# Second pass of an attention and mixer kernel: relus two products later, three raw results in other tiles, weights rounded earlier, weight sums spread over two groups

## The chip, the cores and the metric

The kernel runs on one core of a Trainium2 chip. Five engines work beside each other, each through its own queue in order: TensorE (PE; its weight loads are PEld), VectorE (DVE), ScalarE (ACT), GpSimd (POOL) and SyncE (SP), which here issues the DMAs. Matrix products go from SBUF to PSUM; the other engines empty PSUM and add tiles in SBUF. The metric is the time of one launch on the device in microseconds (us). [...]

## The reference, cut to what matters

```
# attention: q, k, v are (8, 8, 576, 64)
kv  = einsum('bhsd,bhse->bhde', k, v)
out = einsum('bhsd,bhde->bhse', q, kv)
out = out / sqrt(mean(out * out, -1) + 1e-6) * g_norm
x   = out.transpose(0, 2, 1, 3).reshape(8, 576, 512)
# mixer
h = relu(x.T @ w_tok1) @ w_tok2      # over the tokens, 576 -> 256 -> 576
u = x + h.T
return u + relu(u @ w_ch1) @ w_ch2   # over the channels, 512 -> 1536 -> 512
```

The four weights are given as 64-bit floats, the rest is 32-bit.

## The kernel before, in words

**First pass (0 to about 254 us).** Attention and token mixing for pairs of batches; u goes to DRAM (`u_dram`). The order on each engine is chosen by a scheduler from the order in which the code is written and from its own costs, so the diff does not show it. In the same stretch the weights come in as pairs of 32-bit words and are rounded to 32-bit floats by `decode` (lines 142 to 165), one block of 128 rows at a time. There are 16 blocks of `w_ch1` and 12 of `w_ch2`. A block is one DMA into a tile `raw` (three turn), one instruction of ScalarE (line 154), two of GpSimd (155, 165) and four of VectorE (157, 159, 161, 163). The steps of the blocks are woven among the steps of the pass (`weave`, line 632): fetch of a block ahead of the rounding of the block before it.

**Second pass (254 us to the end).** Nine groups of 512 tokens (the ninth holds the last 64 tokens of all eight batches) go through the channel mixer: u @ w_ch1, relu, @ w_ch2. All instructions that go through `keep` (line 111) stay in the order of the code on their engine. The products are done by Winograd's form of Strassen's scheme: 7 products of blocks, called by their numbers in the order 1, 6, 7, 5, 2, 3, 4, in place of 8, with sums of blocks ahead of and behind them.

- `channel1_once` (line 429), group 0: one level of the scheme, in 3 parts, 21 products.
- `channel1` (line 490), groups 1 to 8: two levels. Each of seven outer products `o` is itself seven inner products, the functions `first` (1), `sixth`, `seventh`, `fifth`, `second`, `fourth`, `third`. An inner product is 3 matmuls of 128x128 into a PSUM tile of the pool `m`, which has six. Behind it ScalarE copies it (`t1`, and the quarter `dst(0, 0)`) or VectorE adds it (`u2`, `u3` and the other three quarters of the result).
- The result of an outer product is a raw tile `v` or `vs`: a11, a12, a22, s1 to s4 (printed as v11, v12, v22, vs1 to vs4). GpSimd adds such tiles to each other (`padd`, six sums of 128x1536 a group). ScalarE takes relus of a11, a22 and a12 in place, and VectorE then forms s1, s2, s3, s4 (`v_sums`, `v_sum3`), the operands of channel2.
- `channel2` (line 572): 7 products, the operands `V[g]`, results added into `xg` by VectorE; the transposes of the next group's u (`prepare`) stand between its products.

A relu is put into ScalarE's queue not where its sum is, but in the last step of the next outer product (`later`, lines 496 and 564):

```
            def third():
                product(3, "p5", False, True)
                tensor_add(dst(0, 1), at["p5"], at["u2"])
                while relus:
                    relus.pop()()
                after()
```

The two-level scheme needs sums of the weights: seven blocks `w2` for the outer level, made in the first pass, 28 sums for the inner level (`mix_ch1_of`, tile `w1`, in part in place in `w_ch1` and `w2`), and 8 sums of `w_ch2` (`mix_ch2`, tile `d2`). All are VectorE instructions. In group 0 the rounding of the last four blocks of `w_ch2` (with tiles of their own, `stage2`) and the 8 sums of `mix_ch2` are woven among the 21 products of `channel1_once`; the 28 sums stand behind the 7 steps of group 0's `channel2`, four behind each.

Of the kernel before, what the change touches and what calls it, by code (L numbers as in the profile page):

```python
# [9 lines left out]
F32 = mybir.dt.float32  # L10
# [7 lines left out]
def kernel(  # L18
# [123 lines left out]
    def decode(dst, raw):  # L142

        lo, hi = raw[..., 0], raw[..., 1]
        bits = dst.bitcast(U32)
        part = late.get("stage", stage).tile(list(dst.shape), F32, name="part", tag="part", bufs=2)
        keep(nc.scalar.activation(dst, hi.bitcast(F32), AF.Copy, scale=2.0 ** -112))
        nc.gpsimd.tensor_scalar(out=dst, in0=dst, scalar1=TOP, scalar2=-TOP,
                                op0=ALU.min, op1=ALU.max)
        keep(nc.vector.tensor_scalar(out=bits, in0=bits, scalar1=3, scalar2=None,
                                     op0=ALU.logical_shift_left))
        keep(nc.vector.scalar_tensor_tensor(out=bits, in0=hi, scalar=0x80000000, in1=bits,  # L159
                                            op0=ALU.bitwise_and, op1=ALU.bitwise_or))  # L160
        keep(nc.vector.tensor_scalar(out=part.bitcast(U32), in0=bits, scalar1=0xFF800000,  # L161
                                     scalar2=None, op0=ALU.bitwise_and))
        keep(nc.vector.scalar_tensor_tensor(out=part, in0=lo, scalar=2.0 ** -52, in1=part,  # L163
                                            op0=ALU.mult, op1=ALU.mult))
        nc.gpsimd.tensor_tensor(out=dst, in0=dst, in1=part, op=ALU.add)
# [4 lines left out]
    def block(n, loads, dst, turn=lambda raw: raw, home=None):  # L170

        raw = []

        def fetch():
            if home is None:
                raw.append(late.get("stage", stage).tile([P, n, 2], U32, name="raw", tag="raw", bufs=3))
            else:
                raw.append(home.tile([P, n, 2], U32, name="raw", tag="h1"))
            for o, i in loads(raw[0]):
                nc.sync.dma_start(o, i)  # L180

        return fetch, lambda: decode(dst, turn(raw[0]))
# [53 lines left out]

    def mix_ch2():

        steps = []
        for i in range(2):  # L240
            t1, t2, t4 = (late["d2"][:, n, ts(i, NS // 2)] for n in range(3))
            b11, b12, b21, b22 = (w_ch2[:, n, ts(i, NS // 2)] for n in range(4))
            steps.append([do(tensor_add, o, a, b, ALU.subtract)
                          for o, a, b in ((t1, b12, b11), (t2, b22, t1), (b12, b12, b22),
                                          (t4, b21, t2))])
        return [step for pair in zip(*steps) for step in pair]

    def w2_of(n):
        i = {1: 0, 7: 1, 2: 2, 3: 3}
# [240 lines left out]
    def channel1(g):  # L490

        a11, a12, a22, s1, s2, s3, s4 = v_blocks(g)
        padd = lambda o, a, b: tensor_add(o, a, b, engine=nc.gpsimd)
        relus = []

        def later(t):
            relus.append(do(relu, t, t))


        def after5():  # L500
            padd(s3, a22, s1)
            padd(a22, a22, a12)
            later(a22)

        def after2():
            padd(a11, a11, s2)
            later(a11)

        def after4():
            v_sums(s1, s2, s3, a11, a22)  # L510
# [4 lines left out]


        plan = {1: (a11, lambda: None), 6: (s1, do(padd, s1, s1, a11)),
                7: (a12, do(padd, a12, a12, s1)), 5: (a22, after5), 2: (s2, after2),
                3: (s4, do(padd, s3, s3, s4)), 4: (s4, after4)}

        def outer(o):
            to, after = plan[o]
# [30 lines left out]
            def second():  # L553
                product(2, "p1", False, True)
                copy(dst(0, 0), at["p1"])

            def fourth():
                product(4, "p7", False, True)
# [2 lines left out]
            def third():  # L561
                product(3, "p5", False, True)
                tensor_add(dst(0, 1), at["p5"], at["u2"])
                while relus:
                    relus.pop()()
                after()

            return [first, sixth, seventh, fifth, second, fourth, third]
# [89 lines left out]
    def run(order, *stages):  # L658
# [6 lines left out]
    tok = [get_tok1(0, 2), get_tok1(2, 2), get_tok1(4, 1)] + [get_tok2(t) for t in range(NTOK)]  # L665
    weights = ([get_ch1(c, f) for f in range(4) for c in range(NC)]
               + [get_ch2(f) for f in range(NF)])
    early, in_group = staggered(weights[:24]), staggered(weights[24:])
    cut = 38
    for fetch, _ in tok:  # L670
        fetch()
# [1 line left out]
    steps = []  # L673
    for pair in range(B // 2 - 1):
        steps += run(both, attention(pair + 1), token_mixing(pair))
    weave(steps, early[:cut])


    left.close()
# [2 lines left out]
    late["u"] = pool("u", 1)  # L682
    fetch_u(0)
    woven = []
    weave([do(woven.append, f) for f in early[cut:]],
          [do(woven.append, f) for f in mix_ch1()])
    steps = run(last, token_mixing(3))
    extra = prepare(0, lambda: ps["o"].tile([P, NC, P], F32, name="ps_ut", tag="o"))
# [8 lines left out]
    late["d2"] = pool("d2", 1, "right").tile([P, 3, NS, DH], F32, name="d2")  # L697
    late["m"] = pool("m", 6, space=bass.MemoryType.PSUM)
    late["t"] = pool("t", 2, space=bass.MemoryType.PSUM)
    for g in range(NG):  # L700
        fetch_u(g + 1)
        extra = prepare(g + 1, t_psum)
        if g == 0:
            with ExitStack() as late_stage:
                late["stage"] = pool("stage2", 2, "right", late_stage)
                weave(channel1_once(g), in_group + mix_ch2())
            late["w1"] = pool("w1", 1, "right").tile([P, 4, 3, FQ], F32, name="w1")
            sums = [mix_ch1_of(o) for o in ORDER]
        else:
            for step in channel1(g):  # L710
                step()
            sums = [[]] * 7
        for n, step in enumerate(channel2(g)):
            step()
            for f in extra[n:n + 1] + sums[n]:
                f()


# [33 lines left out]
```

## Time and profile before

| | |
|---|---|
| median of 3 runs | 943.27 us (940.22 to 946.04) |
| the profiled execution, time | 948.9 us |
| its span | 947.1 us |
| granted TensorE clock, mean | 0.971 |
| PE busy | 868.9 us, 92% |
| VectorE busy | 558.9 us, 59% |
| GpSimd busy | 273.0 us, 29% |
| ScalarE busy | 176.3 us, 19% |
| chain that ended last: PE / DVE / POOL | 63% / 17% / 10% |

The profile is of one execution; its span runs from the first instruction to the last, and the time of the execution is 1.8 us more. Its time lies 5.6 us above the median of the three runs. Busy shares are means over both passes: the rows of single stretches further below tell what binds where. An "idle before" is the time for which the engine had nothing running ahead of this group of instructions, with what ended most of it.

### The profile page before, as it was taken

The page shows a single profiled execution, that of the slowest core. Times are in us where ns is not written, and L with a number is a line of the kernel's source. Part 1 is how long each engine was busy: PE and PEld are TensorE (multiplying, and loading weights), DVE is VectorE, ACT ScalarE, POOL GpSimd, SP SyncE. Part 2 cuts the span into 40 slices and gives each one's busy share as a digit, 9 for nine tenths or more (in the row PEclk, how much of TensorE's full clock was granted, in tenths as well). Part 3 has the DMA queues.
Part 4 walks back from the last instruction along what each step waited for, and adds up shares of the span by engine and source line. Part 5 has one row for each costly group of instructions (what it writes and reads, how often), then busy time and mean ns, then how long its engine had stood idle before and what let it go on. Part 6 is the DMA issues. An engine that isn't in the chain of part 4 may idle for free.

```text
span 947.1 us, 12401 instructions
## 1 busy us (share of the span) xinstructions
PE 868.9 (92%) x5136; PEld 737.6 (78%) x5136; DVE 558.9 (59%) x862; ACT 176.3 (19%) x300; POOL 273.0 (29%) x144
## 2 busy tenths in 40 slices
PE   4699969879999988998999999899899899899897
PEld 4565555554587888898898889789789889889886
DVE  1868688786477664464554546536636546446551
ACT  2132222221121012112102202301211211210310
POOL 1534454552030017007106104303501600700710
PEclk9799979979999989999999999999999999999999
DMA  8787858624200020020011001002002002001001
GB/s 271 226 291 267 285 167 266 201 90 144 101 23 0 10 81 2 1 90 1 1 48 43 1 23 67 1 1 90 1 1 89 2 0 90 1 1 45 2 1 44
DMA packets 43576, 72.53 MB, mean 77 GB/s; under 512 B 2688, under 2 KB 21120, under 8 KB 43520
## 3 DMA queue, kind: packets, MB, share of 16 engines
q1 hardware_dynamic: 43376, 71.71, 22.8%
q8 instruction: 40, 0.66, 0.3%
q14 instruction: 16, 0.13, 0.0%
q10 hardware_dynamic: 144, 0.03, 0.0%
HBM read 52.85 MB, written 18.87 MB: 76 GB/s over the span
## 4 chain that ended last, share of the span: by engine, by line
PE 63%; DVE 17%; POOL 10%; issue 4%; DMA 3%; ACT 2%; POOLq 0%; SPq 0%; DVEq 0%; ACTq 0%
PE ps_w L124 33%; PE ps_v L124 21%; POOL vs L115 5%; POOL v L115 3%; PE ps_kv L266 2%; PE ps_u L345 2%; PE ps_h L327 2%; DVE w_ch L159 2%; PE ps_ut L378 2%; DVE part L161 1%; DVE ms L281 1%; DMA raw<-in_moe_w_ch_dram 1%; DVE x L294 1%; DVE part L163 1%; DVE u L115 1%
## 5 line engine op out<-in xcount | busy, mean ns | idle before, releaser
L124 PE MATMUL ps_v<-uT,w 128*128 128x128 f32 (+1 forms) x1656 | 221.6, 287 | 26.6 <-ACT t L121 18.1
L124 PEld LDWEIGHTS ps_v<-uT,w 128*128 128x128 f32 x1656 | 206.3, 197 | 33.6 <-ACT t L121 19.7
L115 POOL TENSOR_TENSOR vs<-vs,v 128x1536 f32<-128x1536 f32 x8 | 27.5, 3442 | 414.3 <-DVE vs L115 414.3
L124 PE MATMUL ps_v<-uT,w_ch 128*128 128x128 f32 (+1 forms) x864 | 126.6, 290 | 5.1 <-DVE u L115 5.1
L124 PEld LDWEIGHTS ps_v<-uT,w_ch 128*128 128x128 f32 x864 | 114.1, 195 | 9.4 <-DVE u L115 5.7
L124 PE MATMUL ps_w<-d,vs 128*128 128x256 f32 x432 | 96.2, 379 | 0.0
L124 PE MATMUL ps_w<-w_ch,v 128*128 128x256 f32 x432 | 96.2, 379 | 0.0
L124 PE MATMUL ps_w<-w_ch,vs 128*128 128x256 f32 x432 | 96.2, 379 | 0.0
L124 PEld LDWEIGHTS ps_w<-w_ch,vs 128*128 128x128 f32 x432 | 81.5, 190 | 10.7
L124 PEld LDWEIGHTS ps_w<-w_ch,v 128*128 128x128 f32 x432 | 80.8, 190 | 10.3
L124 PEld LDWEIGHTS ps_w<-d,vs 128*128 128x128 f32 x432 | 80.8, 190 | 10.3
L115 DVE TENSOR_TENSOR u<-ps_v,t 128x384 f32<-128x384 f32 (+1 forms) x59 | 33.3, 564 | 78.8 <-PE ps_v L124 44.2
L115 DVE TENSOR_TENSOR vs<-ps_v,u 128x384 f32<-128x384 f32 (+1 forms) x99 | 54.9, 561 | 39.8 <-PE ps_v L124 23.5
L266 PE MATMUL ps_kv<-v_in,k_in 128*128 128x128 f32 x320 | 49.4, 322 | 30.2 <-ACT kvp L270 20.9
L266 PEld LDWEIGHTS ps_kv<-v_in,k_in 128*128 128x128 f32 x320 | 46.6, 233 | 37.8 <-ACT kvp L270 24.1
L121 ACT COPY t<-ps_v 128x384 f32<-128x384 f32 (+1 forms) x59 | 28.4, 481 | 192.1 <-PE ps_v L124 192.1
L118 ACT ACTIVATE v<-v 128x1536 f32<-128x1536 f32 (+1 forms) x30 | 39.4, 1314 | 115.1 <-DVE v L115 83.9
L115 DVE TENSOR_TENSOR v<-ps_v,u 128x384 f32<-128x384 f32 (+1 forms) x78 | 44.3, 568 | 25.1 <-PE ps_v L124 19.9
L345 PE MATMUL ps_u<-h,w_tok 128*128 128x512 f32 x128 | 58.8, 603 | 0.0
L115 POOL TENSOR_TENSOR v<-v,vs 128x1536 f32<-128x1536 f32 x16 | 55.0, 3440 | 10.3 <-DVE v L115 10.3
L327 PE MATMUL ps_h<-x,w_tok 128*128 128x512 f32 x128 | 57.4, 595 | 0.3 <-POOL x L295 0.3
L295 POOL TENSOR_TENSOR x<-x,g_sb 128x1024 f32<-128x1024 f32 (+1 forms) x20 | 44.6, 2231 | 44.0 <-DVE x L294 28.9
(79 smaller groups left out, 977.5 us busy)
## 6 DMA issues: line engine op xcount, KB each, us to landing
qT<-in_q_dram SPq DMA_DIRECT2D x8, 1152.0 KB, 7.2
xg<-u_dram SPq DMA_DIRECT2D x9, 1024.0 KB, 5.7
k_in<-in_k_dram SPq DMA_DIRECT2D x16, 512.0 KB, 4.8
v_in<-in_v_dram SPq DMA_DIRECT2D x16, 512.0 KB, 6.3
u_dram<-x SPq DMA_DIRECT2D x16, 512.0 KB, 3.2
out_dram<-xg SPq DMA_DIRECT2D x16, 512.0 KB, 2.8
raw<-in_moe_w_ch_dram SPq DMA_DIRECT2D x16, 384.0 KB, 5.7
raw<-in_moe_w_ch_dram SPq DMA_DIRECT2D x12, 512.0 KB, 5.9
```

Source lines behind the costliest of these rows:

```text
L115: keep(engine.tensor_tensor(out=o, in0=a, in1=b, op=op))
L118: keep(nc.scalar.activation(o, a, AF.Relu))
L121: keep(nc.scalar.copy(o, a))
L124: keep(nc.tensor.matmul(*a, **kw))
L159: keep(nc.vector.scalar_tensor_tensor(out=bits, in0=hi, scalar=0x80000000, in1=bits, op0=ALU.bitwise_and, op1=ALU.bitwise_or))
L161: keep(nc.vector.tensor_scalar(out=part.bitcast(U32), in0=bits, scalar1=0xFF800000, scalar2=None, op0=ALU.bitwise_and))
L163: keep(nc.vector.scalar_tensor_tensor(out=part, in0=lo, scalar=2.0 ** -52, in1=part, op0=ALU.mult, op1=ALU.mult))
L266: nc.tensor.matmul(acc[:, i], lhsT=kk[:, j, ts(i, P)], rhs=vv[:, j, ts(i, P)], start=(j == 0), stop=(j == JJ - 1))
L295: nc.gpsimd.tensor_mul(x3, x3, g_sb.to_broadcast([P, n * H, D]))
L327: nc.tensor.matmul(acc[side, t], lhsT=w_tok1[:, j, ts(t, P)], rhs=x_of(pair, side * J + j), start=(j == 0), stop=False)
L345: nc.tensor.matmul(acc_u, lhsT=w_tok2[:, t, ts(i % J, P)], rhs=h1[i // J][:, t], start=(t == 0), stop=(t == NTOK - 1))
L378: keep(nc.tensor.transpose(pt[:, c], xg[g][:, i, ts(c, P)], ident))
```

## The change

Three things change, all in the order or place of work; the sums, products and relus are the same in number, and so are the bytes moved.

1. In `channel1` the result of o=5 goes to s3 in place of a22, that of o=2 to s4 in place of s2, and that of o=3 to s2 in place of s4. The two GpSimd sums behind o=5 change places: first a22 = s3 + a12, then s3 = s3 + s1. The relu of a22 is put in behind the second step of o=3 that fills `p1` (`second`), and that of a11 in the same step of o=4; before they were in the last step of o=2 and of o=3.
2. All 28 weight blocks are rounded in the first pass; none is left for group 0. The tiles `raw` and `part` of the last four come from the pool of the first pass.
3. Of the 8 sums of `mix_ch2`, four are woven into group 0's `channel1_once`. The other four and the 28 of `mix_ch1_of` make one list. Its first 24 are woven into group 0's `channel2` (its 7 steps and the 6 of `prepare`), the last 8, those of o=3 and o=4, into the first 18 of the 49 steps of group 1's `channel1`.

```
-        part = late.get("stage", stage).tile(list(dst.shape), F32, name="part", tag="part", bufs=2)
+        part = stage.tile(list(dst.shape), F32, name="part", tag="part", bufs=2)
...
-        steps = []
+        firsts, lasts = [], []
...
-            steps.append([do(tensor_add, o, a, b, ALU.subtract)
-                          for o, a, b in ((t1, b12, b11), (t2, b22, t1), (b12, b12, b22),
-                                          (t4, b21, t2))])
-        return [step for pair in zip(*steps) for step in pair]
+            sub = lambda o, a, b: do(tensor_add, o, a, b, ALU.subtract)
+            firsts += [sub(t1, b12, b11), sub(t2, b22, t1)]
+            lasts += [sub(b12, b12, b22), sub(t4, b21, t2)]
+        return firsts, lasts
...
         def after5():
-            padd(s3, a22, s1)
-            padd(a22, a22, a12)
-            later(a22)
+            padd(a22, s3, a12)
+            padd(s3, s3, s1)
+            relus.append((3, do(relu, a22, a22)))

         def after2():
-            padd(a11, a11, s2)
-            later(a11)
+            padd(a11, a11, s4)
+            relus.append((4, do(relu, a11, a11)))
...
-                7: (a12, do(padd, a12, a12, s1)), 5: (a22, after5), 2: (s2, after2),
-                3: (s4, do(padd, s3, s3, s4)), 4: (s4, after4)}
+                7: (a12, do(padd, a12, a12, s1)), 5: (s3, after5), 2: (s4, after2),
+                3: (s2, do(padd, s3, s3, s2)), 4: (s4, after4)}
...
             def second():
                 product(2, "p1", False, True)
                 copy(dst(0, 0), at["p1"])
+                while relus and relus[0][0] == o:
+                    relus.pop(0)[1]()
...
                 tensor_add(dst(0, 1), at["p5"], at["u2"])
-                while relus:
-                    relus.pop()()
                 after()
...
-    early, in_group = staggered(weights[:24]), staggered(weights[24:])
+    weights = staggered(weights)
...
-    weave(steps, early[:cut])
+    weave(steps, weights[:cut])
...
-    weave([do(woven.append, f) for f in early[cut:]],
+    weave([do(woven.append, f) for f in weights[cut:]],
...
+    firsts, sums = mix_ch2()
...
-                weave(channel1_once(g), in_group + mix_ch2())
+            weave(channel1_once(g), firsts)
             late["w1"] = pool("w1", 1, "right").tile([P, 4, 3, FQ], F32, name="w1")
-            sums = [mix_ch1_of(o) for o in ORDER]
...
+            sums += [step for o in ORDER for step in mix_ch1_of(o)]
+
+            weave([step for pair in zip(channel2(g), extra + [lambda: None]) for step in pair],
+                  sums[:-8])
+            continue
+        weave(channel1(g), sums[-8:] + [lambda: None] * 14 if g == 1 else [])
```

**ScalarE, end of `channel1` of group 1** (t1 is the copy that frees a PSUM tile, first of an outer product; v11, v22, v12 are a11, a22, a12). Before, from the copy `t1` of o=2 to that of channel2:

```order
L121 COPY t1_2058<-ps_v1_2061 128x384
L121 COPY vs2_1911<-ps_v1_2061 128x3x128
L118 ACTIVATE v22_1909<-v22_1909 128x1536
L121 COPY t1_2095<-ps_v1_2098 128x384
L121 COPY vs4_1913<-ps_v1_2098 128x3x128
L118 ACTIVATE v11_1907<-v11_1907 128x1536
L121 COPY t1_2132<-ps_v1_2135 128x384
L121 COPY vs4_1913<-ps_v1_2135 128x3x128
L118 ACTIVATE v12_1908<-v12_1908 128x1536
L121 COPY t1_2177<-ps_w1_2173 128x512
```

and now:

```order
L121 COPY t1_2054<-ps_v1_2057 128x384
L121 COPY vs4_1901<-ps_v1_2057 128x3x128
L121 COPY t1_2090<-ps_v1_2093 128x384
L121 COPY vs2_1899<-ps_v1_2093 128x3x128
L118 ACTIVATE v22_1897<-v22_1897 128x1536
L121 COPY t1_2127<-ps_v1_2130 128x384
L121 COPY vs4_1901<-ps_v1_2130 128x3x128
L118 ACTIVATE v11_1895<-v11_1895 128x1536
L118 ACTIVATE v12_1896<-v12_1896 128x1536
L121 COPY t1_2173<-ps_w1_2169 128x512
```

The relu of a22 stood between o=2 and the copy `t1` of o=3; it is now two copies later, and the relu of a11 directly ahead of that of a12.

**GpSimd, the six sums of group 1**, before:

```order
L115 TENSOR_TENSOR vs1_1910<-vs1_1910,v11_1907 128x1536
L115 TENSOR_TENSOR v12_1908<-v12_1908,vs1_1910 128x1536
L115 TENSOR_TENSOR vs3_1912<-v22_1909,vs1_1910 128x1536
L115 TENSOR_TENSOR v22_1909<-v22_1909,v12_1908 128x1536
L115 TENSOR_TENSOR v11_1907<-v11_1907,vs2_1911 128x1536
L115 TENSOR_TENSOR vs3_1912<-vs3_1912,vs4_1913 128x1536
```

and now:

```order
L115 TENSOR_TENSOR vs1_1898<-vs1_1898,v11_1895 128x1536
L115 TENSOR_TENSOR v12_1896<-v12_1896,vs1_1898 128x1536
L115 TENSOR_TENSOR v22_1897<-vs3_1900,v12_1896 128x1536
L115 TENSOR_TENSOR vs3_1900<-vs3_1900,vs1_1898 128x1536
L115 TENSOR_TENSOR v11_1895<-v11_1895,vs4_1901 128x1536
L115 TENSOR_TENSOR vs3_1900<-vs3_1900,vs2_1899 128x1536
```

The sum that completes v22 is third in place of fourth, and the last reads vs2 in place of vs4.

**VectorE, start of group 1** (xg is the output of group 0, w1, w2 and w_ch1 weight sums, u2 and u3 adds that free PSUM tiles). Before, from the last add into xg:

```order
L115 TENSOR_TENSOR xg_1344<-ps_w5_1744,xg_1344 128x2x256
L115 TENSOR_TENSOR w1_1740<-w_ch1_100 128x384
L115 TENSOR_TENSOR w1_1740<-w1_1740,w_ch1_100 128x384
L115 TENSOR_TENSOR w_ch1_100<-w_ch1_100 128x384
L115 TENSOR_TENSOR w1_1740<-w_ch1_100,w1_1740 128x384
L115 TENSOR_TENSOR u2_1915<-ps_v6_1922,t1_1914 128x384
L115 TENSOR_TENSOR u3_1916<-ps_v7_1927,u2_1915 128x384
```

From the last add into xg to u3 of o=1 both orders have these same seven instructions. Behind them now, from the third of the eight late sums on:

```order
L115 TENSOR_TENSOR w2_1337<-w2_1337 128x384
L115 TENSOR_TENSOR u2_1941<-ps_v6_1948,t1_1940 128x384
L115 TENSOR_TENSOR w2_1337<-w2_1337 128x384
L115 TENSOR_TENSOR u3_1942<-ps_v7_1954,u2_1941 128x384
L115 TENSOR_TENSOR vs1_1898<-ps_v5_1959,u3_1942 128x3x128
L115 TENSOR_TENSOR w1_1732<-w_ch1_100 128x384
L115 TENSOR_TENSOR vs1_1898<-ps_v7_1954,u2_1941 128x3x128
L115 TENSOR_TENSOR vs1_1898<-ps_v5_1959,u2_1941 128x3x128
L115 TENSOR_TENSOR w1_1732<-w1_1732,w_ch1_100 128x384
L115 TENSOR_TENSOR u2_1980<-ps_v6_1987,t1_1979 128x384
L115 TENSOR_TENSOR w_ch1_100<-w_ch1_100 128x384
```

Before, no weight sum stood among the adds of group 1; now there are eight.

**VectorE, end of the first pass** (x is the normalized attention output or u, ps_o and ps_u their PSUM tiles). Before:

```order
L294 TENSOR_TENSOR x_1248<-ps_o_1239,inv_1255 128x1024
L354 TENSOR_TENSOR x_982<-ps_u_1279,x_982 128x512
L354 TENSOR_TENSOR x_982<-ps_u_1308,x_982 128x512
L281 TENSOR_REDUCE ms_1296<-x_1294 128x16
L354 TENSOR_TENSOR x_894<-ps_u_1321,x_894 128x512
```

and now:

```order
L163 SCALAR_TENSOR_TENSOR part_1527<-raw_1492,part_1527 128x512
L295 TENSOR_TENSOR x_1248<-ps_o_1239,inv_1255 128x1024
L355 TENSOR_TENSOR x_982<-ps_u_1308,x_982 128x512
L157 TENSOR_SCALAR w_ch2_101<-w_ch2_101 128x2x256
L159 SCALAR_TENSOR_TENSOR w_ch2_101<-raw_1518,w_ch2_101 128x2x256
L161 TENSOR_SCALAR part_1539<-w_ch2_101 128x512
L163 SCALAR_TENSOR_TENSOR part_1539<-raw_1518,part_1539 128x512
L355 TENSOR_TENSOR x_894<-ps_u_1321,x_894 128x512
L282 TENSOR_REDUCE ms_1296<-x_1294 128x16
```

The rounding of the last blocks of w_ch2 stands between the adds that end the pass.

## Rows read from the trace of the kernel before

**Rows 1.** Stretches: length, busy us of PE, PEld, DVE, ACT, POOL; clock; DMA share; GB/s.

```profile
253.91:295.62 41.71, 38.60 (x171) 33.03 (x170) 30.63 (x47) 9.14 (x16) 8.56 (x8) 0.96 0.10 32
333.63:377.42 43.79, 38.44 (x296) 37.67 (x295) 23.91 (x44) 9.55 (x16) 20.58 (x6) 0.88 0.10 37
377.42:904.93 527.51, 504.27 (x3349) 468.71 (x3347) 283.43 (x399) 96.16 (x154) 144.17 (x42) 0.99 0.07 27
604.78:679.82 75.04, 71.64 (x480) 66.53 (x479) 40.50 (x57) 13.75 (x22) 20.60 (x6) 1.00 0.08 29
679.82:717.84 38.02, 38.02 (x187) 33.48 (x185) 20.92 (x22) 4.20 (x6) 0.00 (x0) 1.00 0.04 14
```

**Rows 2.** Timeline, one undisturbed group: start us, length us, instruction, idle before and its end.

```profile
735.46 0.48 ACT L121 COPY v<-ps_v 128x384 f32<-128x384 f32 x1 [2.20 <-PE ps_v L124]
...
736.60 0.83 PE L124 MATMUL ps_v<-uT,w_ch 128*128 128x128 f32 x6
...
737.50 3.44 POOL L115 TENSOR_TENSOR vs<-v,vs 128x1536 f32<-128x1536 f32 x1 [1.23 <-PE ps_v L124]
...
744.40 3.45 POOL L115 TENSOR_TENSOR v<-v,vs 128x1536 f32<-128x1536 f32 x1
744.50 1.48 ACT L118 ACTIVATE v<-v 128x1536 f32<-128x1536 f32 x1 [3.87 <-POOL v L115]
...
746.40 0.94 PE L124 MATMUL ps_v<-uT,w 128*128 128x128 f32 x6 [2.27 <-ACT t L121]
...
753.48 1.02 DVE L115 TENSOR_TENSOR vs<-ps_v,u 128x384 f32<-128x384 f32 x2 [1.54 <-POOL vs L115]
...
754.09 0.94 PE L124 MATMUL ps_v<-uT,w 128*128 128x128 f32 x6 [0.81 <-DVE vs L115]
```

**Rows 3.** Timeline of PE, group 0 and the start of group 1.

```profile
255.75 1.89 PE L124 MATMUL ps_v<-uT,w 128*128 128x256 f32 x8
257.47 1.89 PE L124 MATMUL ps_v<-uT,w_ch 128*128 128x256 f32 x8
...
290.37 2.75 PE L124 MATMUL ps_v<-uT,w_ch 128*128 128x256 f32 x8 [2.33 <-DVE u L115]
...
339.93 1.65 PE L124 MATMUL ps_v<-uT,w_ch 128*128 128x128 f32 x6 [2.79 <-DVE u L115]
```

**Rows 4.** Waits of PE in the second pass: total us, times, longest.

```profile
PE ps_v L124 <- ACT t L121: 18.1, 8, 2.3
```

**Rows 5.** Timeline of VectorE and GpSimd around 225 us.

```profile
223.97 3.73 POOL L295 TENSOR_TENSOR x<-x,g_sb 128x1024 f32<-128x1024 f32 x1 [5.87 <-issue]
...
225.53 3.79 DVE L115 TENSOR_TENSOR w<-w,w_ch 128x1536 f32<-128x1536 f32 x1
```

**Rows 6.** By line, rounding of weights: busy us, mean ns, idle; last, DMA us to landing.

```profile
L165 POOL TENSOR_TENSOR w_ch<-w_ch,part 128x384 f32<-128x384 f32 (+1 forms) x28 | 33.6, 1200 | 45.2 <-DVE part L163 38.2 <-DVE ms L289 6.3 <-DVE ms L282 0.6
...
L163 DVE SCALAR_TENSOR_TENSOR part<-raw,part 128x384 f32<-128x384 uint32 (+3 forms) x33 | 24.6, 749 | 0.4
...
L159 DVE SCALAR_TENSOR_TENSOR w_ch<-raw,w_ch 128x384 uint32<-128x384 uint32 (+1 forms) x28 | 21.1, 760 | 0.5
...
L157 DVE TENSOR_SCALAR w_ch<-w_ch 128x384 uint32<-128x384 uint32 (+1 forms) x28 | 19.3, 696 | 19.3 <-POOL w_ch L155 19.3
...
L155 POOL TENSOR_SCALAR w_ch<-w_ch 128x384 f32<-128x384 f32 (+1 forms) x28 | 18.2, 655 | 60.0 <-ACT w_ch L154 60.0
...
L154 ACT ACTIVATE w_ch<-raw 128x384 f32<-128x384 f32 (+1 forms) x28 | 17.0, 605 | 30.3 <-DMA raw<-in_moe_w_ch_dram 30.2
...
L161 DVE TENSOR_SCALAR part<-w_ch 128x384 uint32<-128x384 uint32 (+1 forms) x28 | 13.7, 495 | 0.3
...
raw<-in_moe_w_ch_dram SPq DMA_DIRECT2D x12, 512.0 KB, 5.9
```

**Rows 7.** Timeline of PE late in the first pass.

```profile
194.74 4.63 PE L266 MATMUL ps_kv<-v_in,k_in 128*128 128x128 f32 x20 [8.52 <-ACT kvp L270]
...
215.76 2.02 PE L302 MATMUL ps_o<-kvp,qT 128*128 128x128 f32 x16 [0.47 <-DVE x L294]
```

More of the change, by code (lines that the diff above doesn't have):

```diff
@@ L175, in fetch @@
             if home is None:
-                raw.append(late.get("stage", stage).tile([P, n, 2], U32, name="raw", tag="raw", bufs=3))
+                raw.append(stage.tile([P, n, 2], U32, name="raw", tag="raw", bufs=3))
             else:
@@ L494, in channel1 @@
         relus = []
-        def later(t):
-            relus.append(do(relu, t, t))
         def after5():
-            padd(s3, a22, s1)
-            padd(a22, a22, a12)
-            later(a22)
+            padd(a22, s3, a12)
+            padd(s3, s3, s1)
+            relus.append((3, do(relu, a22, a22)))
         def after2():
-            padd(a11, a11, s2)
-            later(a11)
+            padd(a11, a11, s4)
+            relus.append((4, do(relu, a11, a11)))
         def after4():
@@ L703 @@
         if g == 0:
-            with ExitStack() as late_stage:
-                late["stage"] = pool("stage2", 2, "right", late_stage)
-                weave(channel1_once(g), in_group + mix_ch2())
+            weave(channel1_once(g), firsts)
             late["w1"] = pool("w1", 1, "right").tile([P, 4, 3, FQ], F32, name="w1")
-            sums = [mix_ch1_of(o) for o in ORDER]
[L709 to L712, printed above, removed]
+            sums += [step for o in ORDER for step in mix_ch1_of(o)]
[3 more added lines that the diff above has]
+        weave(channel1(g), sums[-8:] + [lambda: None] * 14 if g == 1 else [])
         for n, step in enumerate(channel2(g)):
             step()
-            for f in extra[n:n + 1] + sums[n]:
+            for f in extra[n:n + 1]:
                 f()
```

## The prediction

> **What bounds the kernel now.** I read the profile in four steps: the stretches of the second pass, the waits of TensorE, one group in order of time, and last the first pass. TensorE is the bound. In an undisturbed group it is busy for 71.64 of 75.04 us, and all its idle time lies in the first half of the group: the second half, channel2, takes 38.02 us and TensorE is busy in all of them [rows 1]. An outer product of channel1 lasts 4.69 us: four of them pass from 717.84, where a stretch of [rows 1] ends, to 736.60 [rows 2]. So seven outer products need 32.83 us, one inner product 0.67 us, and a group without a wait would need 32.83 + 38.02 = 70.85 us. The group lasts 75.04, as do the one ahead of it and the three behind it to within 0.01: **4.19 us are lost in each**.
>
> The same comparison elsewhere [rows 1]: groups 2 to 8, from the start of channel2 of group 1 to that of group 8, take 527.51 us where 7 x 70.85 = 495.95 would do, 31.6 over. Channel1 of group 1 takes 43.79 against 32.83, 11.0 over. Channel1 of group 0 has 21 products of 1.72 us each [rows 3], 36.1 us, and takes 41.71, 5.6 over. That is 48.2 us in all, and the change can win no more than that in the second pass. [...]
>
> The waits say who holds TensorE: above all the copy `t` on ScalarE, once in each of the 8 two-level groups, 18.1 us [rows 4]. The group in order of time [rows 2] says why. The fourth outer product (o=5) ends at 736.60. GpSimd starts its sum into s3 at 737.50, and only behind it the one that completes a22, done at 744.4. The relu of a22 stands in ScalarE's queue and waits 3.87 us for it, until 744.50. Behind it stands the copy that frees the PSUM tile of the next outer product. TensorE was due to go on at 736.60 + 4.69 + 4 x 0.67 = 743.97 and goes on at 746.40: 2.43 us. The late VectorE adds cost another 0.59 at the next product, and near the end TensorE waits 0.97 (due 753.12, starts 754.09) for adds into s4 that wait 1.54 themselves, since GpSimd still reads s4. 0.20 goes into refilling behind the two waits; together 4.19.
>
> **Relus and tiles.** Nothing is computed more or less; the work moves. GpSimd's first sum behind o=5 now completes a22, at 737.50 + 3.44 = 740.94. Its relu stands five products later, where it finds its input done: no wait, and 2.43 + 0.59 + 0.10 go. The result of o=3 goes to s2, so s4 is last read by the sum into a11, which ends as now at 744.40 + 3.45 = 747.85; o=4 first writes s4 after its fourth product, at 748.66. So the 0.97 + 0.10 goes too, with 0.8 us to spare. What is late next is the relu of a11. It now stands in o=4 behind the copy of the second product. That copy starts 1.14 us before an outer product ends (735.46 for 736.60), so at 749.53 for an o=4 that ends at 750.67; with 0.48 for the copy and 1.48 for the relu [rows 2] it is done at 751.55. Channel2 begins with a product that reads a11: a **new wait of 0.9, with refilling 1.0 us a group**. Queued behind that relu are only the relu of a12 and the next copy, needed a product later; VectorE loses nothing, as the last sum into s3 ends at 747.85 + 3.44 = 751.3, when o=4's last add does. Its bounds are 0.8 and 3.4 (one GpSimd add late). Groups 2 to 8 keep 7 x 1.0 = 7.0 of their 31.6.
>
> **Clock.** Group 1 has 0.88, the seven behind it 0.99 together, the undisturbed one 1.00, though the 2.43 us wait stands in all; I let what the clock cost go with the wait. [...]
>
> **No rounding in the second pass.** Group 0 waits 2.33 us for a VectorE add `u` that stands behind weight work [rows 3]. Four blocks leave VectorE there. Four differences of weights stay between its products; an add has two products, 3.4 us, before TensorE needs it. I take 0 left of the 5.6, with 1 as the other end.
>
> **Weight sums.** [...] New are the eight sums between the adds of group 1. Such a sum reads two SBUF tiles. In [rows 5] a sum of such a form took 3.79 us: it started beside a GpSimd instruction and, it seems, ran only when that had ended at 227.70, since 1.62 are left from there. The first GpSimd add of group 1 (3.44 us) starts where three of the eight are queued; one sum runs ahead of it, the next stands behind it with the adds of o=7 in its back. I take 2.9 us, between 0 and 3.4. Group 1 keeps 3.0 + 3.5 + 2.9 + 1.0 = 10.4 of 11.0.
>
> **The first pass** takes in the four blocks: 4 x (0.696 + 0.760 + 0.495 + 0.749) = 10.8 us on VectorE, 7.4 on GpSimd, 2.4 on ScalarE [rows 6], and their transfers, three of which went there already. VectorE sets two waits of TensorE there [rows 7]. The 8.52 us one is for copies behind rounding: between the normalization and that copy stand 11 such instructions instead of 14, at a mean of 0.675 us that is 2.0 less. Behind it, the normalization that releases the last scores comes eight instructions, 5.4 us, later, where now TensorE waits 0.47; TensorE does some 2 us of products before these scores that it did after them. Net I take **+2 us**, between -4 (waits shorter, half-speed work behind them gone) and +10.8 (all exposed).
>
> **Sum.** 48.2 - 7.0 - 10.4 = 30.8 won in the second pass, 2 given in the first: 28.8. The profiled execution took 948.9, so 920.1. The median of the runs shown, 943.27, lies 5.6 below it; at that distance the new median is 914.5, **915 us**.
>
> **Rivals.** (1) *The first pass pays in full.* For it: VectorE is its busiest helper and the rounding stands ahead of normalizations. Against it: VectorE has idle time there. [...] (2) *The relu of a11 becomes the old wait.* It could start at 750.01 and its sum is done at 747.85; if GpSimd runs more than 2.2 us late, TensorE waits as now. [...] (3) *The change moves the wait and does not remove it*, ScalarE finding other inputs undone: 4.19 a group stays, 5.6 won in group 0, 4.9 lost beside it: 943. The times in [rows 2] speak against it. (4) *Slower:* the extra blocks share the three landing tiles of the first pass instead of having their own. One block takes 5.9 to land [rows 6], 0.605, 0.655 and 2.70 to be rounded, 9.9 us. If they go one behind the other, the pass ends 4 x 9.9 = 39.5 later: 943.3 + 39.5 - 30.8 = 952. With three tiles turning it is 3.3 us a block and hidden; it decides from where only one turns.
>
> **Numbers.** Forecast 0.73, (1) 0.13, (2) 0.07, (3) 0.04, (4) 0.03. The forecast's own range is 904 (first pass 4 shorter, no wait at group 1's start) to 924 (smaller clock gain, new waits at their upper half). To leave out no more than 2 in 10 the range goes to 931. One per cent, about what a measurement of this kernel can tell from no change, is 933.8 and 952.7. Faster 0.88, same 0.09, slower 0.03.
>
> **What would show it.** An undisturbed group of 71.9 us; TensorE's wait for `t` gone from the table of waits, and a wait of channel2's first product for the relu of `v` in its place, eight times; ScalarE's relu not waiting for GpSimd; group 0's channel1 at 36 us; a sum `w` of over 3 us at the start of group 1; channel1 of group 0 starting at 256 instead of 253.9. The forecast is wrong if the group stays above 74, or if that start moves past 262.

## The result and the profile after

The changed kernel took 920.43 us in the median of 4 runs (919.83 to 920.95); the kernel before, run beside it, 941.96 (940.22 to 946.04). The ratio is 0.9765, with a 95% interval of 0.973 to 0.980: faster. The forecast was 915, with a range of 904 to 931. The profiled execution of the changed kernel took 920.95, its span is 919.2, its mean granted clock 0.981 (0.971 before); the profile prints the clock of TensorE as a share, 1.00 at the most in all stretches read here. Beside the experiments below the kernel before was run 34 more times; one of these runs took 1131.09 us at a mean clock of 0.75 and is left out of every comparison.

First the stretches of the changed kernel, cut at the same places of the program as [rows 1]: channel1 of group 0, channel1 of group 1, groups 2 to 8, one undisturbed group and the channel2 behind it.

```profile
259.98:296.34 36.36, 36.36 (x170) 32.02 (x169) 18.41 (x27) 7.33 (x12) 0.00 (x0) 1.00 0.06 22
334.36:374.45 40.09, 35.41 (x295) 34.65 (x293) 29.43 (x52) 9.47 (x16) 20.76 (x6) 0.96 0.11 41
374.45:876.91 502.46, 497.78 (x3347) 464.70 (x3347) 284.24 (x400) 95.64 (x154) 144.19 (x42) 1.00 0.08 28
589.79:661.57 71.78, 71.11 (x478) 66.39 (x478) 40.60 (x58) 13.66 (x22) 20.61 (x6) 1.00 0.09 30
661.57:699.69 38.12, 38.12 (x184) 33.59 (x185) 20.33 (x21) 4.20 (x6) 0.00 (x0) 1.00 0.04 14
```

Against [rows 1], group 0 wins 5.35, channel1 of group 1 wins 3.70, groups 2 to 8 win 25.05: 34.1 us together (the rest of the second pass changes by 0.1). The first number of the first row says what was given back: channel1 of group 0 starts at 259.98 where it started at 253.91, **6.07 later**. 34.1 - 6.07 is the 28.0 us by which the two profiled executions differ (948.9 and 920.95).

The waits of TensorE in the second pass of the changed kernel (total, times, longest) answer to [rows 4]:

```profile
PE ps_w L124 <- ACT v L118: 5.3, 8, 0.7
PE ps_v L124 <- DVE u L115: 4.0, 2, 2.1
```

The wait for the copy `t` is gone. In its place stands the forecast wait of channel2's first product for a relu of `v`, eight times 0.67. The timeline of the undisturbed group of the changed kernel answers to [rows 2] (start, length, instruction, idle before):

```profile
646.67 0.83 PE L124 MATMUL ps_v<-uT,w_ch 128*128 128x128 f32 x6
...
647.60 3.45 POOL L115 TENSOR_TENSOR v<-vs,v 128x1536 f32<-128x1536 f32 x1 [1.25 <-DVE vs L115]
...
654.54 3.45 POOL L115 TENSOR_TENSOR v<-v,vs 128x1536 f32<-128x1536 f32 x1
654.91 0.48 ACT L121 COPY vs<-ps_v 128x384 f32<-128x384 f32 x1 [2.20 <-PE ps_v L124]
655.29 1.49 ACT L118 ACTIVATE v<-v 128x1536 f32<-128x1536 f32 x1
...
659.66 0.48 ACT L121 COPY vs<-ps_v 128x384 f32<-128x384 f32 x1 [2.26 <-PE ps_v L124]
660.03 1.49 ACT L118 ACTIVATE v<-v 128x1536 f32<-128x1536 f32 x1
...
661.57 1.13 PE L124 MATMUL ps_w<-w_ch,v 128*128 128x256 f32 x4 [0.67 <-ACT v L118]
```

GpSimd's first sum behind o=5 (647.60) now writes `v`, which is a22. Its relu at 655.29 waits for nothing: it follows its copy at once. The relu of a11 (660.03) stands behind the copy of 659.66, though its sum was done at 654.54 + 3.45 = 657.99, and TensorE waits until the relu ends.

In group 1 the timeline of the changed kernel shows the two waits that are left:

```profile
339.94 0.94 PE L124 MATMUL ps_v<-uT,w_ch 128*128 128x128 f32 x6 [2.07 <-DVE u L115]
...
340.88 5.62 PE L124 MATMUL ps_v<-uT,w 128*128 128x128 f32 x48
...
347.24 3.62 POOL L115 TENSOR_TENSOR vs<-vs,v 128x1536 f32<-128x1536 f32 x1 [112.21 <-DVE vs L115]
347.95 0.56 DVE L115 TENSOR_TENSOR u<-ps_v,t 128x384 f32<-128x384 f32 x1 [0.39 <-PE ps_v L124]
...
348.42 2.85 DVE L115 TENSOR_TENSOR w_ch<-w_ch 128x384 f32<-128x384 f32 x1
...
351.19 0.55 DVE L115 TENSOR_TENSOR u<-ps_v,u 128x384 f32<-128x384 f32 x1
...
351.80 0.94 PE L124 MATMUL ps_v<-uT,w_ch 128*128 128x128 f32 x6 [1.95 <-DVE u L115]
...
352.57 7.15 PE L124 MATMUL ps_v<-uT,w 128*128 128x128 f32 x48
```

The second is the one that the prediction took from [rows 5]: a weight sum that takes 0.55 us elsewhere takes 2.85, since it started beside GpSimd's sum and ended 0.41 us after that did (347.24 + 3.62 = 350.86). The add of 347.95, which reads a PSUM tile, kept its 0.56 beside the same GpSimd sum. The add `u` behind the weight sum is late, and TensorE waits 1.95. The 48 matmuls behind that wait take 7.15 us where the 48 of 340.88 took 5.62: the granted clock from 351.80 to 360.00 is 0.79; from 339.94 to 351.80, behind the first wait, it is 1.00.

For the first pass, the waits of TensorE in the kernel before, and below them those of the changed kernel:

```profile
PE ps_kv L266 <- ACT kvp L270: 20.9, 6, 8.5
PE ps_o L302 <- DVE x L294: 10.1, 3, 8.7
...
PE ps_h L327 <- POOL x L295: 0.3, 1, 0.3
```

```profile
PE ps_kv L267 <- ACT kvp L271: 15.7, 6, 6.0
PE ps_o L303 <- DVE x L295: 15.4, 4, 8.7
...
PE ps_h L328 <- POOL x L296: 1.5, 2, 1.2
PE ps_o L303 <- ACT kvp L271: 1.2, 1, 1.2
```

The waits for `kvp` fall by 5.2 as forecast in kind. Those for the normalization `x` grow by as much, and 2.4 of others come on top. The largest growth lies at 96 us, far ahead of the places that the prediction looked at. The scores there in the kernel before:

```profile
94.28 2.02 PE L302 MATMUL ps_o<-kvp,qT 128*128 128x128 f32 x16 [0.89 <-DVE x L294]
```

and in the timeline of the changed kernel, with the two places of [rows 7] as they are now at its end:

```profile
90.97 0.56 DVE L163 SCALAR_TENSOR_TENSOR part<-raw,part 128x384 f32<-128x384 uint32 x1
91.45 1.21 DVE L282 TENSOR_REDUCE ms<-x 128x16 f32<-128x1024 f32 x1
...
95.09 1.22 DVE L295 TENSOR_TENSOR x<-ps_o,inv 128x1024 f32<-128x1024 f32 x1
...
96.46 3.64 PE L303 MATMUL ps_o<-kvp,qT 128*128 128x128 f32 x16 [4.04 <-DVE x L295]
...
196.38 4.64 PE L267 MATMUL ps_kv<-v_in,k_in 128*128 128x128 f32 x20 [5.96 <-ACT kvp L271]
...
222.07 2.02 PE L303 MATMUL ps_o<-kvp,qT 128*128 128x128 f32 x16 [1.70 <-DVE x L295]
```

The four instructions that round a block (the last of them is shown) now end right ahead of a normalization: its first instruction starts at 91.45 where it started at 88.81, and the scores that wait for it start 2.2 us later. TensorE also reaches them 1.0 us earlier than before, in another order of its products, so the wait grows from 0.89 to 4.04. The 16 matmuls behind it take 3.64 us where they took 2.02: their granted clock is 0.53, and 1.00 for those of the kernel before. At the two places that the prediction weighed, 8.52 became 5.96 (the 20 matmuls behind it take 4.64 us at 0.50, 4.63 at 0.51 before) and 0.47 became 1.70.

### The profile page after: what moved, and what is told of

Read it like the earlier page. It is cut to its first block, busy times and chain, and to the rows that moved or that the text cites. A ratio compares the mean times of both kernels' runs of the same rounds, so it can differ in the third digit from the quotient of the medians.

```text
span 919.2 us, 12409 instructions
## 1 busy us (share of the span) xinstructions
PE 860.9 (94%) x5136; PEld 731.5 (80%) x5136; DVE 564.3 (61%) x862; ACT 176.3 (19%) x300; POOL 273.6 (30%) x144
## 4 chain that ended last, share of the span: by engine, by line
PE 73%; DVE 14%; DMA 3%; issue 3%; ACT 3%; POOL 2%; SPq 0%; ACTq 0%; DVEq 0%
PE ps_w L124 35%; PE ps_v L124 31%; PE ps_u L346 2%; DVE w_ch L159 2%; PE ps_ut L379 2%; DVE ms L282 2%; DVE part L161 1%; DVE part L163 1%; POOL x L296 1%; DMA v_in<-in_v_dram 1%; PE ps_h L328 1%; DVE w_ch L157 1%; PE ps_kv L267 1%; ACT v L118 1%; DMA raw<-in_moe_w_tok_dram 1%
## 5 line engine op out<-in xcount | busy, mean ns | idle before, releaser
L124 PE MATMUL ps_v<-uT,w 128*128 128x128 f32 (+1 forms) x1656 | 211.3, 281 | 0.0
L124 PEld LDWEIGHTS ps_v<-uT,w 128*128 128x128 f32 x1656 | 199.9, 193 | 2.0 <-DVE v L115 0.2
L124 PE MATMUL ps_v<-uT,w_ch 128*128 128x128 f32 (+1 forms) x864 | 124.2, 287 | 4.0 <-DVE u L115 4.0
L115 DVE TENSOR_TENSOR vs<-ps_v,u 128x384 f32<-128x384 f32 (+1 forms) x123 | 69.0, 561 | 39.3 <-PE ps_v L124 30.4
L115 DVE TENSOR_TENSOR u<-ps_w,u 128x512 f32<-128x512 f32 x18 | 12.4, 692 | 73.6 <-PE ps_w L124 73.6
L115 DVE TENSOR_TENSOR uT<-uT 128x512 f32<-128x512 f32 (+1 forms) x68 | 56.7, 874 | 0.9 <-ACT uT L121 0.3
```

What stands on the lines that cost most here:

```text
L115: keep(engine.tensor_tensor(out=o, in0=a, in1=b, op=op))
L124: keep(nc.tensor.matmul(*a, **kw))
```

## The experiments

**The theory**: each part acts in its own stretch and the parts add up. The relus and tiles carry the whole gain; the early rounding costs more in the first pass than it wins in group 0; the spread sums cost in group 1. **The rival**: the parts need each other, so that the relus alone win less than the whole.

**1. Relus and tiles alone.** The kernel before, with `channel1` of the changed kernel.

```
 in the kernel before:
+            padd(a22, s3, a12)
+            padd(s3, s3, s1)
+            relus.append((3, do(relu, a22, a22)))
...
 (the rest of channel1 as in the diff above; rounding and weight sums as before)
```

> Only part 1 (tiles, order of the GpSimd sums, places of the relus) put into the kernel before. [...] Rival B, the parts need each other (the early rounding pays for itself and more): 921 us or above.

Measured: 914.44 us (912.98 to 917.49), ratio to the kernel before 0.9703 (0.9671 to 0.9736). The stretches of group 0 and group 1 (channel1) of this run:

```profile
253.22:293.24 40.02, 36.90 (x171) 31.86 (x169) 30.15 (x47) 8.97 (x16) 8.55 (x8) 1.00 0.10 33
331.25:367.96 36.71, 33.26 (x295) 32.87 (x293) 24.54 (x46) 9.46 (x16) 20.61 (x6) 1.00 0.13 44
```

Groups 2 to 8 take 502.46, as in the whole change. This one part wins 27 us, more than all three. Channel1 of group 1 takes 36.71 (43.79 in [rows 1]): the wait at its start is there with 2.79, but the granted clock is 1.00, and the six matmuls behind the wait take 0.94 where [rows 3] has 1.65, at a granted 0.50. The same holds for group 0: 40.02 without any change of the work there, where [rows 1] has 41.71 at 0.96.

**2. Early rounding alone.**

```
...
-    early, in_group = staggered(weights[:24]), staggered(weights[24:])
+    early, in_group = staggered(weights), []
...
-                weave(channel1_once(g), in_group + mix_ch2())
+            weave(channel1_once(g), mix_ch2())
```

> Only part 2 (all 28 blocks rounded in the first pass) put into the kernel before; the 8 sums of w_ch2 all stand in group 0. Theory A: the first pass ends at 260 as in the changed kernel, channel1 of group 0 takes 36 to 37, groups 2 to 8 stay at 527: a gain of 5 and a cost of 6, 941 to 944 us, no difference that can be told from the 942 before. Rival: the rounding costs less in the first pass without the rest, 937 or below.

Measured: 944.92 us (943.83 to 949.66) beside 941.65, ratio 1.0038 (1.0020 to 1.0055): slightly slower, just above what the theory gave. The first pass ends at 260.57; channel1 of group 0 takes 36.37 at a clock of 1.00. TensorE's wait at the scores of 96 us is 4.03 in this run and 0.89 in run 1, which rounds as the kernel before does: it is the early rounding that makes it. Channel1 of group 1 and groups 2 to 8 of this run:

```profile
334.95:376.15 41.20, 35.37 (x295) 34.64 (x294) 23.82 (x44) 9.45 (x16) 20.61 (x6) 0.96 0.12 40
376.15:901.37 525.22, 501.50 (x3349) 465.84 (x3348) 283.41 (x399) 96.27 (x154) 144.16 (x42) 1.00 0.08 27
```

Here all seven groups last 75.02 to 75.05, with every wait of [rows 4] still in place: the 2.2 us by which groups 2 to 8 in [rows 1] last longer than seven undisturbed ones (527.51 - 7 x 75.04), at a granted 0.99, belonged to that one execution, not to the kernel. The same holds for 2.6 of the 43.79 us that channel1 of group 1 takes there: its work is the same here, and it takes 41.20.

**3. Relus, tiles and early rounding, sums as before** (run 2 with the `channel1` of run 1).

```
+            weave(channel1_once(g), mix_ch2())
             late["w1"] = pool("w1", 1, "right").tile([P, 4, 3, FQ], F32, name="w1")
             sums = [mix_ch1_of(o) for o in ORDER]
```

> Parts 1 and 2, without part 3: the 8 sums of w_ch2 in group 0, the 28 sums behind the steps of group 0's channel2, none in group 1. [...] Rival: the spreading of the sums is worth something, 922 or above.

Measured: 917.80 us (916.64 to 918.30), ratio 0.9736 (0.9704 to 0.9769). Channel1 of group 1 in this run:

```profile
333.38:370.09 36.71, 33.25 (x296) 32.87 (x294) 24.55 (x46) 9.46 (x16) 20.61 (x6) 1.00 0.12 44
```

The changed kernel has 40.09: spreading the sums costs 3.4 us in that stretch, of which 1.5 is the 48 matmuls behind its second wait (7.15 for 5.62). It is not the clock of one execution alone, since in runs 4, 5 and 7, which spread the sums too, the stretch takes 41.16, 39.26 and 41.45. Of the whole times the intervals of the ratios overlap (0.9765 for the change), so it is the stretch that shows it. Run 1 to run 3 is the early rounding again: 3.4 us.

**4. The relus back at their old places, tiles and sums as changed.**

```
             def second():
...
-                while relus and relus[0][0] == o:
-                    relus.pop(0)[1]()
...
             def third():
                 product(3, "p5", False, True)
                 tensor_add(dst(0, 1), at["p5"], at["u2"])
+                while relus:
+                    relus.pop(0)[1]()
                 after()
```

> The changed kernel with the relus of a22 and a11 back in the last step of o=2 and o=3 (ahead of the copy t of the next outer product); tiles and order of the GpSimd sums as changed. Theory A, by the times of the changed kernel: the relu of a11 waits there for its sum (done 657.99), runs to 659.48, and the copy t behind it to 659.96; TensorE, due at 658.73, waits 1.2, then 0.5 for the late VectorE add, while the wait of channel2 for a11 goes: a group of 72.7 us where the changed kernel has 71.8 and the kernel before 75.0; 927 to 930 us. Rival B, the place of the relus is the whole gain: groups of 74 or more, 937 us. Rival C, the order of the sums is the whole gain: 71.8 or less, 920 or below.

Measured: 928.95 us (927.53 to 929.52), ratio 0.9851 (0.9823 to 0.9879), and groups of 72.74 or 72.75: theory A. In the timeline of this run:

```profile
734.75 1.48 ACT L118 ACTIVATE v<-v 128x1536 f32<-128x1536 f32 x1 [2.63 <-POOL v L115]
...
736.14 0.46 ACT L121 COPY t<-ps_v 128x384 f32<-128x384 f32 x1
...
736.66 0.94 PE L124 MATMUL ps_v<-uT,w_ch 128*128 128x128 f32 x6 [1.03 <-ACT t L121]
...
737.91 0.94 PE L124 MATMUL ps_v<-uT,w_ch 128*128 128x128 f32 x6 [0.32 <-DVE u L115]
```

The relu of a11 holds up ScalarE's queue for 2.63 us, and the copy behind it holds up TensorE. Of the 3.26 us that a group wins, the order of the sums and the tiles bring 2.3, the places of the relus 1.0. The order and the tiles were not tried apart.

**5. The relus one copy earlier.** The changed kernel, with the relu behind the copy `t` of o=3 and o=4.

```
             def first():
...
                 copy(at["t1"], at["p1"])
+                while relus and relus[0][0] == o:
+                    relus.pop(0)[1]()
...
             def second():
...
-                while relus and relus[0][0] == o:
-                    relus.pop(0)[1]()
```

> The changed kernel with one more move: the relus of a22 and a11 stand behind the copy t at the start of o=3 and o=4, one copy earlier than in the changed kernel. Theory A (the wait of 0.67 us of channel2 for the relu of a11 is a matter of ScalarE's queue alone, since its sum is done 2.0 us before it starts): the relu starts when GpSimd's sum ends, is done 0.2 us before the next copy is due, and the wait is gone in all eight groups: a group of 70.9 us (71.78 in the changed kernel), 912 to 914 us in all. Rival: something else is late next at the start of channel2 (VectorE's sums, the relu of a12, or the copy behind the relu), a group of 71.5 or more, 918 or above.

Measured: 913.86 us (912.95 to 914.72), ratio 0.9700 (0.9660 to 0.9741). One group, as a stretch of this run, and its end in the timeline:

```profile
586.30:657.14 70.84, 70.84 (x480) 66.31 (x479) 40.61 (x58) 13.79 (x22) 20.62 (x7) 1.00 0.09 31
```

```profile
654.42 1.49 ACT L118 ACTIVATE v<-v 128x1536 f32<-128x1536 f32 x1 [0.62 <-POOL v L115]
...
656.00 0.48 ACT L121 COPY vs<-ps_v 128x384 f32<-128x384 f32 x1
...
657.14 4.05 PE L124 MATMUL ps_w<-w_ch,v 128*128 128x256 f32 x18
```

TensorE is busy for all of the group; 70.85 was what the prediction worked out as a group without a wait. The relu starts when its sum ends and is done 0.09 us before the copy behind it.

**6. The late sums placed beside no GpSimd sum.**

```
...
+            sums = sums[-8:]
...
-        weave(channel1(g), sums[-8:] + [lambda: None] * 14 if g == 1 else [])
+        late_at = (3, 5, 7, 9, 11, 13, 20, 20) if g == 1 else ()
+        for n, step in enumerate(channel1(g), 1):
+            step()
+            for at_step in late_at:
+                if at_step == n:
+                    sums.pop(0)()
```

> The changed kernel with the last two or three of the eight late weight sums placed where GpSimd is idle (steps 3, 5, 7, 9, 11, 13, 20, 20 of channel1 of group 1). [...] Rival (the 2.85 us come from the number of adds in VectorE's queue): the wait stays, only elsewhere; 920 us.

Measured: 917.73 us (915.48 to 918.71), ratio 0.9738 (0.9695 to 0.9781). Channel1 of group 1 takes 36.25 (40.09 in the changed kernel). That stretch, and the sum that took 2.85 us with GpSimd's sum in the timeline of this run:

```profile
332.72:368.97 36.25, 33.52 (x295) 32.95 (x293) 27.12 (x52) 9.48 (x16) 20.59 (x6) 1.00 0.14 45
```

```profile
345.86 3.45 POOL L115 TENSOR_TENSOR vs<-vs,v 128x1536 f32<-128x1536 f32 x1 [112.46 <-DVE vs L115]
...
349.39 0.55 DVE L115 TENSOR_TENSOR w_ch<-w_ch 128x384 f32<-128x384 f32 x1
```

It starts when GpSimd's sum is over and takes 0.55. The number of adds is the same: it was the meeting. The second wait is gone; the one at the start of the group, 2.07, stays.

**7. Fewer rounding steps late in the first pass.**

```
-    cut = 38
+    cut = 46
```

> The changed kernel with 46 in place of 38 of the 56 fetch and rounding steps woven among the first three pairs, so that 10 instead of 18 stand in the last stretch of the first pass, as many as in the kernel before. Theory A (the 6 us come from rounding that stands ahead of the last normalizations): the first pass ends at 256 to 258, 917 to 919 us. Rival B (VectorE is short everywhere in that pass, so the waits only move forward): 260 to 263, 920 to 923 us.

Measured: 920.89 us (918.88 to 921.78), ratio 0.9772 (0.9730 to 0.9814): no difference to the changed kernel, and in the range of B. The first pass ends at 259.03, between the two expectations and within what the unchanged order gives from one execution to the next (258.34 to 260.57 in six of them). The wait at the scores of 96 us is still 3.26, and the one before the last scores grew from 1.70 to 2.71. So theory A, that only rounding ahead of the last normalizations costs, is not borne out.

**8 to 11. A version made from these parts**: the rounding in group 0 as before, `channel1` of run 5, 24 of the 28 sums and four of `w_ch2` in channel2 of group 0 so that none stands behind the last add into `xg`, four sums in group 1 ahead of GpSimd's first.

```
-            weave(channel1_once(g), firsts)
+                weave(channel1_once(g), in_group + firsts)
...
-                  sums[:-8])
+                  sums[:-4] + [lambda: None] * 7)
...
+        late_at = (4, 7, 10, 13) if g == 1 else ()
```

> A version made from what the runs showed: rounding as in the kernel before (four blocks in group 0), channel1 as in the run before with the relus behind the copy t, four of the sums of w_ch2 and 24 of the 28 others in channel2 of group 0 so that none stands behind the last add into xg, the last four in steps 4, 7, 10 and 13 of group 1, ahead of GpSimd's first sum. Theory A: first pass 253 to 254, channel1 of group 0 37 to 40, channel1 of group 1 near 33 without its wait of 2.8, groups of 70.9: 914.4 - 7.4 - 2.8 - 1 = 903 us, 900 to 906. Rival: VectorE is too busy in channel2 of group 0 and delays TensorE there by 2 or more, 906 to 910.

Measured: 910.09 us (907.87 to 911.42), ratio 0.9658 (0.9606 to 0.9710). Groups of 70.85 and channel1 of group 1 at 33.75 came as expected, but channel1 of group 0 took 45.73, so the time fell where the rival had put it, but not by its cause: channel2 of group 0 takes 38.02, as before. Group 0 had two waits in this run that neither expectation named:

```profile
275.99 2.70 PE L124 MATMUL ps_v<-uT,w_ch 128*128 128x256 f32 x8 [2.42 <-DVE u L115]
...
293.06 2.71 PE L124 MATMUL ps_v<-uT,w_ch 128*128 128x256 f32 x8 [3.03 <-DVE u L115]
```

With fewer steps to weave, the rounding stood later, next to the four VectorE instructions that end a part. The three versions that follow change the places in group 0 (run 10 also puts all eight sums of `w_ch2` back there):

```
 run 9:  at_step = {3: [r0, f3], 5: [r1], 8: [r2], 10: [r3], 15: firsts[:1],
                    16: firsts[1:2], 17: firsts[2:3], 18: firsts[3:]}   # f0, f1, f2 ahead of step 1
 run 10: weave(channel1_once(g), in_group + <all eight sums of w_ch2, in the order before>)
 run 11: at_step = {3: [r0, f3], 5: [r1], 11: [r2], 17: [r3], 19: firsts[:1],
                    20: firsts[1:2], 21: firsts[2:]}
```

> As the version before it (groups of 70.85, no wait at the start of group 1), but in channel1 of group 0 the rounding stands at steps 3, 5, 8 and 10 with three fetches ahead of step 1, and the four sums of w_ch2 at steps 15 to 18, away from the steps in which VectorE forms the operands of channel2. Theory A (the 45.7 us of group 0 in the version before came from rounding that ran late and met the last steps of the second and third part): channel1 of group 0 takes 36.4 to 38.5, the rest as in the version before, 900 to 903 us. Rival (VectorE's load alone makes the waits of TensorE there, wherever the rounding stands): 40 or more, 904 us and above.

Measured: 903.66 us (902.76 to 904.11), ratio 0.9585 (0.9548 to 0.9623), channel1 of group 0 39.15: between the two expectations, with waits of 1.4 and 0.9 left.

> As the version with groups of 70.85, but with the rounding and all eight sums of w_ch2 woven in group 0 exactly as in the kernel before, and the 28 other sums alone in channel2 of group 0 and in group 1. Theory A: channel1 of group 0 takes 40.0 as in the run with the relus alone (45.7 in the first such version), channel1 of group 1 33 to 34; 904 to 906 us. Rival: the 45.7 came from another cause and stays, 910.

Measured: 903.82 us (903.40 to 904.76), ratio 0.9591 (0.9546 to 0.9637), channel1 of group 0 40.04 and of group 1 33.28: theory A, though the time is just below its 904 to 906.

> The version with rounding at steps 3, 5, 8 and 10 of group 0, with the third and fourth block moved to steps 11 and 17 and the four sums of w_ch2 to steps 19 to 21, so that no rounding stands between VectorE's operands of a part and the first two adds of the next. Theory A (the two waits left in group 0 came from that meeting): channel1 of group 0 takes 36.4 to 37.5 where that version has 39.15, 901 to 902.5 us. Rival (VectorE's load alone): 39 or more, 903.5 and above.

Measured: **899.26 us** (897.52 to 901.21), ratio 0.9522 (0.9488 to 0.9557), the fastest: 4.8% below the kernel before and below the changed kernel by the same comparison (0.9765). It lies below both expectations, theory A's 901 to 902.5 included; group 0 came out as theory A said. Its channel1 of group 0, channel1 of group 1, and groups 2 to 8:

```profile
253.20:289.57 36.37, 36.37 (x171) 32.07 (x170) 26.68 (x42) 9.13 (x16) 7.64 (x8) 1.00 0.11 36
...
327.58:361.34 33.76, 33.09 (x295) 32.90 (x294) 23.37 (x42) 9.56 (x16) 19.95 (x6) 1.00 0.15 48
361.34:857.27 495.93, 495.93 (x3349) 464.45 (x3348) 284.15 (x400) 96.33 (x154) 144.19 (x43) 1.00 0.08 28
```

The rounding of four blocks costs group 0 nothing at these places: 36.37, the same as with no rounding at all. In the whole second pass TensorE waits once, 0.7 us.

## Why the prediction was right, and where its sizes were off

- **Relus and tiles: right.** A group of 71.78 for the forecast 71.9; groups 2 to 8 502.46 for 527.51 - 24.6 = 502.9; the new wait of 0.67 for 0.9, at the place named and with the cause named. (By its own terms, 749.53 + 0.48 + 1.48, the relu was to end at 751.49 and not at 751.55, which makes the wait 0.8.) Runs 1, 4 and 5 bear out the mechanism from both sides.
- **No rounding in group 0: right for that execution.** 36.36 for the forecast 36.1. But 1.7 of the gain was clock: runs 1 and 10 take 40.0 there, at a clock of 1.00, with the old work, so without the fall of the clock the gain is 3.7.
- **Weight sums: right in kind, 3.1 too high.** Channel1 of group 1 keeps 40.09 - 32.83 = 7.3 over, where 10.4 were forecast. The stall beside GpSimd came, with a weight sum of 2.85 us where "over 3" was forecast (1.95 of waiting, and 1.5 for the 48 matmuls behind it, 7.15 for 5.62; 2.9 forecast), and the wait at the start came (2.79 in [rows 3], 2.07 now; 3.0 in the sum). The 3.5 in that sum, for the clock behind this wait, no run shows: the 54 matmuls behind it took 9.05 in the profile of the kernel before and 6.13 in runs 1 and 2, after the same 2.79, which is 2.9, and behind the 2.07 of the changed kernel the granted clock was 1.00.
- **First pass: the step that was mis-sized.** "Net I take +2 us" measured 6.07, and over six executions each the pass ends at 259.7 with all blocks (mean) and at 252.9 without the four, 6.8 apart. The prediction weighed two waits late in the pass, and there it was near: 8.52 became 5.96 (2.0 less was forecast) and 0.47 became 1.70. What it put at nothing, without a reason, are the waits elsewhere: 3.2 more at 96 us, and waits of 0.95, 1.21 and 1.21 at 157, 176 and 235 us that were not there before. They were still there with the rounding put earlier (run 7). Net, TensorE's idle time grew by 2.4, and its busy time by 3.7 (213.16 to 216.82) for the same products. Of these 3.7, 1.6 is the 16 matmuls behind the wait at 96 us (3.64 for 2.02, at a granted 0.53); the rest was not followed up.
- **From the profiled execution to the median: the step that failed.** The sum gave 920.1 for the profiled execution, and that took 920.95. That it came so close is in part luck: the prediction had 3.1 too little won in group 1 and 4.1 too little given back in the first pass, and the two nearly cancel. The prediction then took off the 5.6 us by which the old profile lay above its median, and left the gain whole. The new profile lies 0.5 above its own median. The old distance was the clock in one execution: 33 runs of the kernel before beside the experiments took 938.7 to 948.6 at mean clocks of 0.971 to 0.982, the four slowest at 0.971 to 0.973, and its profile, at 948.9 and 0.971, is slower than all of them. The stretches say how much: with the old work, channel1 of group 0 took 1.7 less in run 1 than in [rows 1], and channel1 of group 1 and groups 2 to 8 took 2.6 and 2.3 less in run 2, 6.6 together. In the median the gain was 21.5, between the profiles 28.0, 6.5 more. The prediction set granted clocks of 0.88, 0.99 and 1.00 in the old profile beside the same wait for `t`, and still let what the clock cost go with the wait; its range took in a smaller gain from the clock, its forecast did not. With the 6.6 us out of the gain the forecast would have been 915 + 6.6 = 921.6.
- **Rivals.** None of the four came. Rival 1, the first pass, came half way: 6 of its 10.8. Run 2 shows what it means: early rounding is a loss of 3.3 us by itself, since it costs 6 to 7 in the first pass, where VectorE holds up TensorE, to save 3.7 in group 0; run 11 saves the same 3.7 by placing.

Two questions stay open: why TensorE's busy time in the first pass grows by more than the stretch at 96 us explains, and whether rounding placed around the normalizations would cost less there, as it did between the products of group 0. Neither was tried.

## What to carry to other kernels

Where an engine in order stands still in front of one instruction, look at what is queued behind it: here a relu that waited 3.9 us cost nothing itself, and the copy behind it cost 2.4 a group. Work that is moved is not free because the engine that takes it has idle time in the mean: ask, stretch by stretch, whether that engine sets a wait there. And take the distance of a profile from its median off only after the clock of that execution has been compared with that of the other runs.

## What the runs showed of the hardware

- In group 1 of the changed kernel a VectorE sum of two SBUF tiles that started while GpSimd added two SBUF tiles did not run beside it: 2.85 us in place of 0.55, ending 0.41 after GpSimd's sum; placed behind GpSimd's sum (run 6) it took 0.55. A VectorE add that reads PSUM kept its 0.56 beside the same GpSimd sum.
- The same waits are followed by different clocks from one execution to the next: channel1 of group 1, with the same work and the same two longest waits (2.8 and 2.2 us), took 43.79 us at a granted 0.88 in the profile of the kernel before and 41.20 at 0.96 in that of run 2; the six matmuls behind the 2.8 took 1.65 in the one and 0.94 in the other.
